# Another order of issue for the same 1303 operations of a delta-rule attention with a softplus layer behind it

## The chip, the cores and the metric

The kernel runs on one core of one Trainium2 chip, in one launch. The metric is device time in microseconds from start to end of that core's program. Engines are named as in the profile: PE is TensorE (matmul), PEld its weight load, DVE is VectorE, ACT is ScalarE, POOL is GpSimd, SP is SyncE, which here only issues DMAs.

## What is computed

```python
def _attn_ref(q, k, v, beta, g):          # 4 batches, 8 heads, 768 tokens, 48 features
    k_n = k / (np.linalg.norm(k, axis=-1, keepdims=True) + 1e-06)
    state = np.zeros((B, H, D, D))
    for t in range(S):
        readout = einsum('bhd,bhde->bhe', q[:, :, t], state)
        y[:, :, t] = g[:, :, t] * readout
        v_old = einsum('bhde,bhd->bhe', state, k_n[:, :, t])
        state = state + beta_t * einsum('bhd,bhe->bhde', k_n[:, :, t], v[:, :, t] - v_old)

def _moe_ref(x, w_in, w_out):             # x: y as 3072 tokens x 384; w_in 384 x 2048, w_out 2048 x 384
    h = x @ w_in
    return softplus(h) @ w_out
```

Each token reads the state of its head before it updates it. The second part is two dense layers with a softplus between them.

## The kernel before

**Tiling.** The 768 tokens are cut in 12 chunks of 64, for all 32 heads (4 batches x 8) at once. Inside a chunk the update of 64 tokens is done as matrix products with the inverse of a triangular matrix of 64 x 64 for each head; from chunk to chunk the state is handed on. The dense layers run on tokens of a chunk as soon as its output is there. Every piece of work is an `Item` with a number, a kind, a tag, the engines that can do it, the items it depends on and the buffers it uses. A letter and a number such as `P658` in the order table mean: issue item 658 now, on engine P (PE), D (DVE), A (ACT), G (POOL) or S (SP). The text names items by kind and tag, for example `ks:1.0` (chunk 1, half 0).

**What the items are**, in the order in which a chunk needs them:

- `load` (L264, L286): one half of a chunk's k, q, v or g, 192 KB, into one of three (k, v, g) or two (q) tiles; `cast` and `kmul` write it in 16 bits; `ksq`, `red`, `sqrt` or `pow` (L582, on POOL), `eps` make the norms of k, for two chunks at a time.
- `trs` and `kev`: transposes on PE and their copies; `gram`, `gramd`, `gramk`, `gramq`: products of k and q with k; `kkc`, `mask`: their copies.
- For each pair of chunks (tag 0, 2, 4, ...) `kd0`, `kd1`, `ln`, `clear`, `diag`, `prep`, then `step:pair.j`: 15 steps (pairs 0 and 2) or 31 steps (pairs 4 to 10) of forward substitution, each a multiply (L661) and an add (L668) that need the step before. A step may be on DVE or POOL. Then `cv`, `tn`, `c16`, `t32`, `xmm`, `xs`, `tmm`, `tlo`, `thi`, `zmm`, `z` build the rest of the inverse.
- The chain of the state, by chunk and half: `ks` (k times the state, L846), `w` (v less that, L887), `umm` (L895), `u1`, `zu` (L918), `u2`, then `smm` (L938) and `s` (the new state), and `qs`, `ymm` (L968), `y` (times g, L983), `ytr`, `xt` for the output. `ks` of the next chunk needs both `s:c.0` and `s:c.1`.
- `g1` (L1032): a piece of x @ w_in; `soft` (L1044, ACT): softplus; `g2` (L1059): four of 16 pieces of the second product, in the order .0, .4, .8, .12 into one PSUM bank; `o` and `store`.
- `wload` (L312, POOL's DMA queue): the eight weight transfers of 384 KB. w0.0 to w0.3 are quarters of w_in, w1.0 to w1.3 of w_out. The `g1` of columns 0 to 3 needs w0.0, and so on; `g2:c.p.0` needs w1.0, `.4` needs w1.1, `.8` w1.2, `.12` w1.3.
- `warm` (L1114): fills, 32 items of three matmuls on the identity whose results nobody reads.

**What sets the order.** `Program.emit` walks the table and calls each item's function, so the table is the order of instructions on each engine. Semaphores hold an instruction back until what it reads is there; an engine takes its own instructions strictly in turn. Buffers are given out in the order of the table too: the first item that uses a buffer takes the slot of the ring that came free first, and waits for that slot's last user. Rings that matter here: three tiles each for k, v and g, two for q, five PSUM banks `d`, two `h`, one `o`.

```python
        for word in table.split():
            en, no = word[0], int(word[1:])
            it = self.items[no]
            assert en in it.engs and no not in done and all(d.no in done for d in it.deps)
            for b in it.bufs:
                if b.ap is None:
                    b.slot = b.ring.free.pop(0)
                    b.ap = b.ring.tiles[b.slot]
            it.fn(en)
```

Of the kernel before, what the change touches and what calls it, by code (L numbers as in the profile page):

```python
# [1136 lines left out]
G259 A292 D293 A294 P651 D652 A206 G260 D261 D295 D262 A622 G263 G264 A207 D296 D312 P913 P316
A317 A914 P654 A655 P658 D659 G265 P300 A301 S64 P297 D298 D266 S63 P919 P166 D170 A920 P307
P921 A310 P313 A375 D311 S66 S65 S35 G267 S81 S82 G268 G269 D168 G270 G271 A922 P302 D306 A314
D304 A308 P1280 A303 D376 A305 P923 P318 D309 P210 D320 P323 A373 A321 A324 P917 A326 A319 A328  # L1140
S30 P1281 D211 G272 D374 P1288 P1290 A918 D273 P279 D325 A274 A924 D329 D330 A280 P1289 P1287
S36 A465 D275 D331 S51 P661 A662 P653 P656 A657 G377 D332 D333 D334 D335 D336 P911 A912 P915
# [6 lines left out]
G361 G362 S87 P1291 P1292 P695 D696 P693 D694 A381 P1293 P385 A386 G363 G364 D387 P927 A388 D389
P697 D698 P390 D392 D394 A481 A393 P690 A391 P689 D691 D692 P928 P929 P930 P288 D395 P708 A931  # L1150
D457 P706 P699 D700 S95 P396 A397 S45 D707 D289 P934 P935 S106 P709 P401 D403 A458 D459 A710
P936 P702 A703 P711 G460 A402 P937 A938 S940 P701 P704 A705 S96 D712 D365 D366 P719 D720 P957
A404 P406 A409 A407 A411 P717 P958 P959 D718 D405 D414 S61 D412 D413 P960 G415 A961 P721 A722
D461 P482 S109 P964 A483 S962 S963 A368 D416 D417 S939 P965 P966 S53 P971 A972 A564 D410 P987
A988 S52 S98 D408 P714 P713 D716 D478 P371 D372 P369 D370 D715 P989 A990 S104 P985 A986 G418
G419 G420 G421 D422 P479 D423 A480 P1001 A1002 P999 P730 P732 P723 D724 A1000 S60 A367 D731 P489
D491 P983 G424 D425 A492 A984 S932 P967 S103 A490 P977 A968 S969 A978 P975 A976 P725 P726 A727
S97 P733 A734 P997 A998 S59 P991 A992 S67 P735 A736 S970 P728 A729 D426 D427 D428 D429 D430 D431
P981 D432 A982 S68 P466 A467 P973 A974 P995 A996 P741 D742 P737 P743 D744 P738 S70 D739 D740
P979 A980 D493 D462 S62 P1003 S933 P745 A746 P747 D748 P484 A485 P754 D755 A541 G433 G434 G435  # L1160
G436 G437 G438 P993 G439 D488 D486 A994 P463 P1004 A464 P757 A758 S69 P750 D487 D542 P1005 P1006
A1007 S1008 P473 P468 D751 A539 D475 D474 P756 P1010 P1011 A469 A471 D540 P759 D470 P1012 S83
P1013 A1014 D760 S1016 P749 P752 A753 S1015 P767 S76 D440 D441 D768 A548 P1017 D472 P765 D766
P761 S84 P762 D764 P1018 G442 G443 G444 A476 G445 G446 G447 P769 P1019 D763 P1020 A494 G543 A770
P565 A1021 A566 P1047 P1031 P1024 D495 D496 A1048 A1032 S78 P1041 A1042 D448 P771 D449 P773
S1023 P778 A451 D779 D477 P1025 P1026 D497 D772 S107 A450 P1053 A1054 P452 P774 P781 D498 A775
P780 P1035 A1036 A782 D453 D499 P1049 P1027 A1028 S1029 P1061 A1050 A1062 D544 P783 A784 P454
P776 A777 D500 P1037 A1038 G501 D561 P562 A563 P1039 A1040 S1009 D502 D503 S1030 P1059 A1060 S75
D504 D505 P789 D506 D507 G508 P567 D571 A570 G509 G510 P791 P1033 A1034 D455 D792 S77 P1057
A1058 A568 D790 P549 A550 P1043 P1045 A1046 D569 P793 A794 D545 P572 A575 D574 D511 G512 P785  # L1170
D576 P786 D788 A1044 A573 D787 P1051 A1052 P546 A547 P1063 P1064 P1055 A1056 P802 P795 D513 D514
P551 A554 A552 P1065 P1066 A1067 S1069 D796 P798 P804 D803 D555 A799 G515 D516 D517 D518 D519
D520 P805 A806 P1070 P1071 P1072 P1073 S94 S1068 A1074 P797 P800 P807 A801 P1077 P1078 D521 A808
P556 P813 G522 D814 P815 A557 A559 P1079 P1080 D816 D558 D553 P817 A1081 S1082 D818 S91 S86 S93
P810 P809 D812 D811 G523 G524 D525 D526 G527 G528 G529 A577 P1084 P1099 G530 P1107 D578 D579
A1100 P828 A1108 P819 S1083 P826 D827 P1109 A1110 P1111 A1112 S110 P1085 P1103 A1104 S85 P1095
A1096 D820 P1086 P1115 A1116 D560 D531 P1117 A1118 D580 G581 D532 A534 D533 P1087 A1088 S1076
S1090 D582 S1089 S99 P1093 A1094 P1091 P829 A830 A1092 P821 P535 P822 A823 S1022 D583 G584 P1121
# [47 lines left out]
```

## Time and profile before

| what | value |
|---|---|
| time, median of 3 runs | 263.37 us (263.04 to 264.32) |
| the profiled execution | 264.15 us, its span 262.4 us |
| mean granted TensorE clock | 0.945 |
| DVE, ACT, POOL busy | 71%, 61%, 45% of the span |
| loads of q, v, g, k | 24 each, 192 KB, 4.7 to 5.0 us to landing in the median |
| weight transfers w_in, w_out | 4 each, 384 KB, 8.1 and 8.0 us |
| stores | 48, 96 KB, 2.4 us |
| PE rows `h` (L1032) and `o` (L1059) | 384 matmuls each, 74.1 and 71.8 us busy |

The span is the time from the first to the last instruction of the profiled execution. "Busy" counts an engine's own instructions; a wait is named with the instruction that ended it. "Granted clock" is the share of full speed that TensorE's throttle lets through.

### The profile page before, as it was taken

What the parts mean: (1) busy time and instruction counts of PE and PEld (TensorE: products, weight loads), DVE (VectorE), ACT (ScalarE), POOL (GpSimd) and SP (SyncE); (2) the same over time, 40 slices, a digit from 0 to 9 for tenths busy, and PEclk for the clock granted to TensorE, in tenths of its full rate; (3) what the DMA queues carried; (4) which work ended last, traced back from release to release, by engine and by line L of the source; (5) the groups of instructions that cost most, each with busy time, mean ns of one, the idle gap of its engine ahead of it and who ended that gap; (6) DMA issues with size and microseconds to landing.
All of it is one profiled execution on the core that took longest, in us unless ns stands there. A gap on an engine that the chain in (4) does not pass through costs nothing.

```text
span 262.4 us, 10491 instructions
## 1 busy us (share of the span) xinstructions
PE 239.2 (91%) x4552; PEld 154.4 (59%) x4552; DVE 186.9 (71%) x417; ACT 161.3 (61%) x297; POOL 118.0 (45%) x190
## 2 busy tenths in 40 slices
PE   6639888498999999999999999999999999999993
PEld 2525554375667676656666566664666455678761
DVE  7999777578988987989977987888566644622100
ACT  3646875298877747889667789455742466046440
POOL 5400983268646288560868735255573442000000
PEclk9658997579999999999999999999999999999998
DMA  8899999859389984895838150228423421012112
GB/s 115 139 181 189 167 185 203 143 103 188 77 158 143 180 128 90 147 178 114 145 69 119 32 106 4 65 54 143 94 49 66 87 50 31 17 32 62 32 45 61
DMA packets 86830, 27.51 MB, mean 105 GB/s; under 512 B 77056, under 2 KB 86784, under 8 KB 86784
## 3 DMA queue, kind: packets, MB, share of 16 engines
q1 hardware_dynamic: 80992, 23.31, 50.4%
q0 software_dynamic: 3712, 3.15, 7.7%
q10 hardware_dynamic: 2080, 0.39, 1.1%
q8 instruction: 35, 0.57, 1.0%
q14 instruction: 11, 0.09, 0.1%
HBM read 25.26 MB, written 4.72 MB: 114 GB/s over the span
## 4 chain that ended last, share of the span: by engine, by line
PE 48%; POOL 15%; DMA 15%; DVE 12%; issue 5%; SPq 2%; ACT 2%; POOLq 0%; DVEq 0%; ACTq 0%
PE o L1059 19%; PE h L1032 15%; DMA kf<-in_k_dram 9%; POOL tmp L661 5%; POOL tt L668 5%; DVE tt L668 4%; DVE tmp L661 4%; DMA w_out<-in_moe_w_out_dram 3%; PE d L846 3%; POOL nv L582 2%; DMA qf<-in_q_dram 2%; PE d L918 2%; PE d L895 2%; PE d L968 2%; PE d L801 1%
## 5 line engine op out<-in xcount | busy, mean ns | idle before, releaser
L1044 ACT ACTIVATE ga<-h 128x512 f16<-128x512 f32 x96 | 56.4, 599 | 32.3 <-PE h L1032 30.8
L1032 PE MATMUL h<-xt,w_in 128*128 128x512 f16 (+1 forms) x384 | 74.1, 331 | 0.0
L1059 PE MATMUL o<-w_out,ga 128*128 128x384 f16 x384 | 71.8, 327 | 1.0 <-ACT osb L203 0.6
L661 POOL TENSOR_TENSOR tmp<-nn,tt 128x192 f32<-128x192 f32 (+19 forms) x73 | 37.4, 512 | 68.2 <-DVE tt L668 64.4
L1059 PEld LDWEIGHTS <-ga 128*128 128x128 f16 x384 | 35.2, 98 | 23.8 <-issue 1.7
L1032 PEld LDWEIGHTS <-w_in 128*128 128x128 f16 x384 | 35.6, 99 | 20.7 <-issue 0.3
L668 POOL TENSOR_TENSOR tt<-tt,tmp 128x192 f32<-128x192 f32 (+19 forms) x73 | 37.9, 520 | 5.7
L661 DVE TENSOR_TENSOR tmp<-nn,tt 128x240 f32<-128x240 f32 (+16 forms) x81 | 26.9, 332 | 13.7 <-POOL tt L668 11.4
L1114 PE MATMUL o<-ident 128*128 128x512 f16 x96 | 28.6, 440 | 1.4 <-POOL ident masks.py:199 1.4
L668 DVE TENSOR_TENSOR tt<-tt,tmp 128x240 f32<-128x240 f32 (+16 forms) x81 | 27.2, 336 | 2.8
L203 ACT ACTIVATE osb<-o 128x384 f32<-128x384 f32 x21 | 10.3, 490 | 25.1 <-PE o L1059 23.7
L203 ACT ACTIVATE kqt<-d 128x1024 f16<-128x1024 f16 (+1 forms) x24 | 21.9, 922 | 3.8 <-PE d L403 1.8
L203 ACT ACTIVATE u<-d 128x384 f16<-128x384 f32 x38 | 17.9, 494 | 6.3 <-PE d L918 3.8
L203 ACT ACTIVATE kk<-d 128x256 f16<-128x256 f32 (+1 forms) x41 | 14.8, 404 | 6.7 <-PE d L518 3.9
L846 PE MATMUL d<-s,kqt 48*64 48x48 f16 x704 | 16.4, 190 | 2.1 <-DVE s L205 2.1
L846 PEld LDWEIGHTS <-kqt 48*64 48x64 f16 x704 | 13.5, 110 | 7.3 <-issue 7.1
L533 DVE TENSOR_TENSOR mt<-d,mask 128x256 f16<-128x256 f32 x40 | 15.5, 417 | 2.5 <-PE d L518 2.1
L582 POOL TENSOR_TENSOR nv<-nv,half_c 128x32 f32<-128x32 f32 x3 | 16.4, 5453 | 0.0
L1114 PEld LDWEIGHTS <-ident 128*128 128x128 f16 x96 | 9.3, 110 | 11.8 <-issue 4.9
L561 ACT ACTIVATE ksq<-kf 128x768 f32<-128x768 f32 x12 | 10.1, 843 | 9.5 <-DMA kf<-in_k_dram 7.5
L983 DVE TENSOR_TENSOR yg<-d,gf 128x384 f16<-128x384 f32 x24 | 12.3, 550 | 3.6 <-PE d L968 3.5
L887 DVE TENSOR_TENSOR w<-vf,d 128x384 f16<-128x384 f32 x22 | 11.3, 543 | 4.4 <-PE d L846 4.4
(116 smaller groups left out, 329.3 us busy)
## 6 DMA issues: line engine op xcount, KB each, us to landing
qf<-in_q_dram SPq DMA_DIRECT2D x24, 192.0 KB, 4.8
vf<-in_v_dram SPq DMA_DIRECT2D x24, 192.0 KB, 4.7
gf<-in_g_dram SPq DMA_DIRECT2D x24, 192.0 KB, 5.0
out_dram<-osb SPq DMA_DIRECT2D x48, 96.0 KB, 2.4
kf<-in_k_dram SPq DMA_DIRECT2D x22, 192.0 KB, 4.7
w_in<-in_moe_w_in_dram POOLq DMA_DIRECT2D x4, 384.0 KB, 8.1
w_out<-in_moe_w_out_dram POOLq DMA_DIRECT2D x4, 384.0 KB, 8.0
kf<-in_k_dram ACTq DMA_DIRECT2D x2, 192.0 KB, 4.6
```

The lines of the kernel that those rows point to most:

```text
L203: nc.scalar.activation(o, x, AF.Copy, scale=float(sign))
L533: nc.vector.tensor_tensor(mt[c][m].ap[:, NP * p : NP * p + NP], gb[m].ap.rearrange("p (n b) -> p n b", n=NP)[:, :, C:], mask[:, None, :].b ...
L582: lambda en: nc.gpsimd.tensor_tensor(nv.ap, nv.ap, half_c, ALU.pow),
L661: ENG[en].tensor_tensor(t, nn_[:, :, j + 1 :, j : j + 1].broadcast_to([P, nb, n, w]), tt_[:, :, j : j + 1, :w].broadcast_to([P, nb, n, w]) ...
L668: ENG[en].tensor_tensor(rows, rows, t, ALU.add)
L846: nc.tensor.matmul(hd(o.ap)[HALF[r], NP * p + i], kq_of(c)[FEAT[m], 8 * p + 2 * i + r, off : off + C], s0[r].ap[FEAT[m], NP * p + i], **st ...
L887: lambda en, m=m, w1=w1, wp=wp: nc.vector.tensor_tensor(w1.ap, heads(vf.ap, m), hd(wp.ap), ALU.subtract),
L983: lambda en, m=m: nc.vector.tensor_tensor(heads(yg.ap, m), hd(yp[m].ap), heads(gf.ap, m), ALU.mult),
L1032: nc.tensor.matmul(hp.ap[:, n * b : n * b + n], w_in[:, j, f * P : (f + 1) * P], xt.ap[:, j, t0 : t0 + n], start=(j == 0), stop=(j == 2),)
L1044: lambda en, hp=hp, o=gb: nc.scalar.activation(o.ap, hp.ap, AF.Softplus),
L1059: nc.tensor.matmul(op.ap[:, :DM], b.ap[:, col + c0 : col + c0 + 128], w_out[:, f, :], start=(f == 0), stop=(f == NF - 1),)
L1114: nc.tensor.matmul(wb.ap.rearrange("p (a b) -> p a b", a=4), ident, ident[:, None, :].broadcast_to([P, 4, P]),)
```

## The change

Only the order table `_ORDER` is replaced. All 1303 items stay, with the same functions, shapes, dependencies and rings. 1277 of the 1303 places hold another word; 110 items change engine, among them 53 steps of the forward substitution (25 from DVE to POOL, 28 from POOL to DVE). The places of the items that the prediction speaks of (a place is the position in the table, from 0; the letter is the engine):

| item | before | after |
|---|---|---|
| `wload:w0.3`, `w0.1`, `w0.2`, `w0.0` | G 191, 207, 155, 169 | G 146, 222, 237, 258 |
| `wload:w1.1`, `w1.3`, `w1.0`, `w1.2` | G 215, 397, 445, 450 | G 429, 379, 431, 432 |
| `load:q4.0`, `q4.1`, `k5.0`, `k5.1` | S 134, 194, 186, 202 | S 158, 164, 186, 185 |
| `load:k7.0`, `k7.1` | S 212, 217 | S 261, 260 |
| `ksq:5`, `ksq:7` | A 237, 277 | A 220, 298 |
| `red:5`, `red:7` | D 238, 298 | D 221, 301 |
| `cv:0` | D 78 | G 75 |
| `kd1:2`, `ln:2` | D 214, 226 | D 212, 213 |
| `s:0.0`, `s:0.1` | D 230, 233 | D 215, 210 |
| `ks:1.0`, `ks:1.1` | P 240, 259 | P 232, 227 |
| `zu:1.0`, `zu:1.1` | P 339, 351 | P 339, 321 |
| `ytr:1.0`, `umm:2.0` | P 372, 432 | P 372, 428 |
| `step:4.13` | G 434 | D 398 |
| `step:4.14` | D 435 | G 399 |
| `g2:0.0.0`, `g2:0.0.8` | P 480, 496 | P 475, 491 |

The first lines of the diff, and those that hold the weight transfers (items 111 to 118) and the two steps 347 and 348:

```diff
 _ORDER = """
-P1271 P1272 G1 S15 P1274 D173 D2 P1273 D3 A16 D126 S10 P129 G4 D125 P127 A24 G623 A119 D120 S12
-S23 A121 D148 S7 S14 S9 D6 S48 S13 P150 S8 S25 G149 P152 S11 D130 G0 P139 S20 A128 P136 S26 D151
...
-A223 A214 D215 S47 A205 P1275 P208 S57 A204 P629 S28 A239 P634 P1276 G113 A216 D209 A630 P631
-A632 D635 P636 G624 S27 D217 D218 P1277 A637 G111 P642 D643 A290 P644 D645 P219 A220 G234 P235
-D236 P646 A647 P648 P224 D649 A227 S55 D226 P240 D244 A241 G114 A225 A243 S50 D228 D242 P245
-A248 D291 P229 A232 S56 D246 P1278 D247 A230 G112 D249 A250 D233 D231 S71 G626 D251 G116 P1279
...
-P281 P278 P383 A952 A285 S37 D344 P945 A384 G118 A946 A398 P955 A956 P665 P666 D668 D667 D379
...
-S105 S54 P953 P947 A948 D676 P678 A679 G347 D348 P1294 D349 P685 A686 D350 D351 P677 P680 A681
-G115 P684 S44 A400 P380 G117 S43 P687 A688 D352 D353 D354 G355 G356 G357 G358 A954 G359 G360
...
+D4 G6 P1271 D173 P1272 S13 G0 G3 A16 S15 D125 P1274 P127 S10 D126 P1273 A24 A119 P129 D120 S23
+D148 D130 S11 S9 S8 S31 S7 A128 P136 D137 S14 S12 A121 D122 S20 S18 A138 P150 G149 P152 P139
...
+P143 D145 D628 S22 P1300 P1301 P1302 S26 A214 D193 A2 G1 S41 P1298 D195 D215 D147 P1295 P196
+A197 A203 G626 A216 D217 D218 A202 P199 A200 P222 P1296 D633 S42 P198 A205 S21 P1297 A204 P208
+P629 A223 P219 A630 A290 D209 D237 G114 P634 A635 G234 P631 A632 P1277 P201 A207 D220 P229 A206
...
+D226 A157 P210 A292 D293 G112 G650 P300 G624 A301 P658 D659 G255 G256 G257 P651 D258 A294 A622
+D295 G113 P166 D259 G260 D296 P661 A662 D261 D262 D263 D264 P925 A926 A373 P297 A298 D168 A315
+D652 P915 A916 G111 P1275 S72 S71 P307 G265 D266 D267 A310 S30 S46 S66 P654 A655 D309 G268 G269
...
+S43 P1289 P673 A674 P1287 D379 P1290 P949 A382 G118 G343 A950 P945 A946 P279 A280 P276 P675 S74
+G625 D344 S73 A277 P941 P953 D345 A954 D346 D347 G348 P383 A384 A942 P278 P281 P943 A285 A284
+S88 P1284 S38 P380 P682 D676 P286 A381 D683 D287 S87 D349 D350 D351 D352 P1283 P1285 S44 P677
+A282 P678 G116 A679 G115 G117 D353 P955 A956 P684 P685 A686 P680 A681 A398 P1286 A458 S81 P1291
...
```

More of the change, by code (lines that the diff above doesn't have):

```diff
@@ L1137 @@
[L1137 to L1142, printed above, removed]
@@ L1149 @@
[L1149 to L1154, printed above, removed]
@@ L1155 @@
[L1155 to L1178, printed above, removed]
@@ new lines @@
+S107 G437 G438 D439 D440 A539 D441 D442 P756 P759 A760 A751 P1006 P749 P767 G443 A1007 P752
+P1010 P1011 S969 P1012 A494 D540 D768 A753 P1013 A1014 S1015 D495 P765 P761 D472 P762 P1017
+P1018 D766 P769 D496 A770 P1019 P1020 A1021 P1055 A1056 G444 G445 G446 G447 D448 D449 D477 S1016
+P1053 A1054 P1024 P1031 S106 P1061 D564 D497 D498 P565 A450 D763 G543 A451 D764 D544 S1023 D499
+P1025 P1026 A566 A1062 S108 S77 S78 P771 D772 P778 D779 P780 D561 P452 A1032 P773 G500 P774 A775
+P1035 D453 A1036 G501 S84 P1041 A1042 G502 D503 S83 D504 D505 D506 P562 D507 D508 P549 P1047
@@ new lines @@
+G597 P1109 P1119 A825 P837 S99 D838 P834 P839 A1110 A1120 P833 D553 P1111 P1117 P1131 A1112
+A1118 D836 P1107 D840 P841 A1108 D835 A842 P843 P850 P852 P1132 P1133 D851 D844 P846 P845 A1134
+D598 D599 D600 P853 A854 S1136 A847 P1123 P1124 D601 G602 G603 P855 A856 G604 P848 A849 P1125
+P1126 A1127 S109 P861 S1135 D862 P857 P858 P863 D859 D864 D605 P1137 P1138 P865 P1139 P1140 A866
+A1141 S1142 P1165 S1143 A1166 P1169 A1170 P1144 D860 P1153 A1154 S1128 P1151 A1152 P1145 P1179
+A1180 P1175 S110 P1146 P1167 A1176 A1168 D606 D607 D608 S1129 G609 G610 G611 G612 G613 P1173
@@ L1196 @@
+P1215 A1216 P1234 P905 P907 D906 P1219 A1220 P1225 A1226 D908 P909 P1221 A1222 P1235 D910 P1249
+A1250 P1243 A1244 P1236 P1237 A1238 S1240 S1239 P1255 A1256 P1247 A1248 P1227 P1241 A1242 P1245
+A1246 P1228 P1229 P1230 A1231 S1232 S1233 P1253 A1254 P1251 A1252 P1257 P1258 P1259 P1260 A1261
+S1262 S1263 P1264 P1265 P1266 P1267 A1268 S1269 S1270
 """
```

69 lines of the change are left out of this document (43 added, 26 removed).

## The prediction

> **What bounds the kernel now.** I read the page first, then the busy time by stretches, then the chain of waits, then single rows.
>
> ```profile
> PE 239.2 (91%) x4552; PEld 154.4 (59%) x4552; DVE 186.9 (71%) x417; ACT 161.3 (61%) x297; POOL 118.0 (45%) x190
> ...
> PEclk9658997579999999999999999999999999999998
> DMA  8899999859389984895838150228423421012112
> ```
>
> TensorE is the bound as a whole, but its clock and the DMA row say that the first 85 us differ from the rest. The stretches (columns: length, busy time and count of PE, PEld, DVE, ACT, POOL, granted clock, DMA share, GB/s):
>
> ```profile
> 42.60:46.00 3.40, 2.06 (x99) 1.60 (x98) 1.90 (x3) 1.57 (x3) 1.36 (x3) 1.00 1.22 198
> 46.00:56.20 10.20, 6.91 (x83) 5.43 (x82) 7.11 (x16) 5.61 (x10) 4.01 (x8) 0.50 0.61 100
> 94.53:126.60 32.07, 32.07 (x677) 20.44 (x677) 28.51 (x58) 24.19 (x44) 18.47 (x30) 1.00 0.70 126
> 126.60:258.30 131.70, 130.28 (x2259) 83.42 (x2257) 79.75 (x170) 73.45 (x132) 52.20 (x87) 1.00 0.33 65
> ```
>
> From 94.5 us on PE hardly idles. So the order is worth what it changes before that: how late PE comes to a given amount of its own work. The chain of waits names two DMA pieces there (start, length, what):
>
> ```profile
> 35.38 14.03 DMA kf<-in_k_dram
> 49.44 0.04 issue
> 49.48 0.85 ACT ksq L561
> ...
> 84.78 0.74 POOL w_out L312
> 85.53 8.96 DMA w_out<-in_moe_w_out_dram
> 94.49 0.04 issue
> 94.53 1.46 PE o L1059 x8
> ```
>
> The rows of the timeline behind them (start, length, engine, line, in brackets the idle time before it and who ended it):
>
> ```profile
> 46.45 0.56 DVE L205 CAST qn<-qf 128x768 f16<-128x768 f32 x1 [1.91 <-DMA qf<-in_q_dram]
> 50.36 0.95 DVE L565 TENSOR_REDUCE nv<-ksq 128x16 f32<-128x768 f32 x1 [2.51 <-ACT ksq L561]
> ...
> 35.20 1.57 POOL L312 DMA_DIRECT2D w_in<-in_moe_w_in_dram  x2
> ...
> 36.90 0.78 POOL L312 DMA_DIRECT2D w_out<-in_moe_w_out_dram  x1
> ...
> 91.75 0.81 PE L1059 MATMUL o<-w_out,ga 128*128 128x384 f16 x4 [0.22 <-DMA w_out<-in_moe_w_out_dram]
> ```
>
> Five weight transfers issued at 31.2 to 36.9 us held back the loads of q4.1 and k5 (k and q loads take 4.7 and 4.8 us in the median), and VectorE idled 1.91 + 2.51 = 4.4 us for them. Later w1.0, issued at 84.72, released the first `o` matmul at 91.75 (7.0 us), and w1.2, at 85.53, the third group at 94.53 (8.96).
>
> **How I count.** The order table is the order on every engine, so the work ahead of an item is a sum of durations. PE items I price by the median distance from start to start in the full stretch: `g1` 0.66, `g2` 0.65, a fill 0.66, `zmm` 0.53, `zu` 0.33, `ymm` 0.29, `umm` 0.27, `ks` 0.26, `gram` 0.25, `smm` 0.23, `qs` 0.21 us; all PE items make 218.4 us. "Offset" is an item's start less the PE work ahead of it. Old: 31.2 at `ks:2.0` (81.6 - 50.4), 32.25 at `g2:0.0.0` (91.75 - 59.5), 33.9 at `ks:5.0`, 39.9 at the end (258.3 - 218.4). The growth after 94 us is spread thin (the largest single piece is 0.74), and no row lets me say that the new order has more or less of it. So the change in time is the change of the offset at `g2:0.0.0`.
>
> **The change part by part.** No operation is added or removed. 110 items change engine, but by their rows the sums are 198.7 to 199.2 us for DVE, 177.3 to 177.6 for ACT, 115.8 to 112.3 for POOL: nothing by itself.
>
> 1. Weights. w0.3 goes from place 191 to 146, w0.1 to 222, w0.2 to 237, w0.0 to 258, w1.1 from 215 to 429. Walking POOL's queue with the durations of its rows, w0.3 is issued near 27 us, while SP waits for a free q tile (`load:q4.0` stands behind `cast:q3.0`, done near 32.7). The q4, v1 and k5 loads then follow at some 0.64 us each, from 32.8 to 37.2, with no weight issued beside them before 41. At the median 4.7 us k5 lands near 42, and ACT comes to its `ksq:5` near 44. So both waits of DVE go: -4.4 us. The bounds are 0 (they are only put elsewhere) and -4.4.
>
> 2. DVE's other waits. Up to step 4.14, at 84.82 us, the old order has 72.7 us of DVE items ahead, so 12.1 us are lost; the new one has the same 72.7. Shuttling steps to POOL and back: by the rows, POOL's part exceeds DVE's cover by 0.62 at step 2.9 and 0.50 at 4.8, and `tn:2` waits 0.74; the new places cover all three: -1.8. Against that, step 0.14 has 16.4 us ahead in place of 17.8 and still ends near 22.8, since its chain starts from the same k loads and casts: +1.4. `cv:0` moves to POOL, 0.94 x 2 in place of 0.35 x 2, +1.2 us on its chain; `red:2`, `mask:0.0` and `w0:0.0` (0.94 + 0.66 + 0.5) fill DVE meanwhile, and behind it on POOL `cast:q2.0`, a fill copy and w0.3 are late by the same. What is late next is `tn:0`, `t32:0`, and all of chunk 0 by about 2 us: `z:0`, `y:0.1`, `kkc:2.01`, `s:0.1` each wait 0.7 to 0.9 where the old order lost 2.6 in all: +1.7. `s:0.0` now stands behind `kd1:2` and `ln:2` (1.29 + 1.04) and starts near 45.6, while the old order was through with both states at 47.5. Lost: 12.1 - 4.4 - 1.8 + 1.4 + 1.7 = 9.0 us, with bounds of 5.9 (none of the pluses) and 12.1 (as before).
>
> 3. The gate at `g2:0.0.0`. In the old order POOL issued w1.0 after step 4.13. In the new one step 4.13 is DVE's, 4.14 is POOL's (0.64 + 0.68), and w1.1, w1.0, w1.2 follow it. DVE ends 4.13 at 72.7 + 9.0 = 81.7, POOL ends 4.14 at 83.2, w1.0 is issued at 84.0, second of three. Its time to landing is bounded by 7.0 (the first of two) and 11.8 (the longest w_out of the issue view, one of five); it is nearest to the second of two, 8.96, which I take: 93.0. PE could be there sooner: DVE's work runs 21.7 us ahead of PE's at `umm:2.0`, so DVE allows an offset of 9.0 + 21.7 = 30.7, or 91 us at 59.9 of work. PE so waits some 2 us; behind it in its queue stand `ks:3` and all of chunk 3, for which DVE's `w:3` wait, with steps 4.15 to 4.30 to do meanwhile. Offset 93.0 - 59.9 = 33.1, against 32.25: **+0.9 us**. The third transfer may land by 95.8 (62.7 + 33.1) without adding to it.
>
> The profiled execution took 264.15 us (span 262.4, 1.75 around it); the sum makes it 265.0. It lay 0.78 above the median of the runs shown, 263.37, so the median becomes **264.2**. The range of this case alone is 262.6 to 266.0: landing 7.0 would give 263.37 - 1.0, and 11.8 would give + 3.7.
>
> **Rivals.**
>
> A. The gate does not bind. Lost time 7.5 (halfway from 9.0 to its lower bound) and w1.0 landing in 7.0 give 84.0 - 1.5 + 7.0 = 89.5, ahead of PE. Then DVE sets the offset: its work is 22.0 ahead of PE's at `ytr:1.0`, so 29.5 there, 30.4 at the gate with the old growth of 0.045 per us over 20 us. 30.4 - 32.25 = -1.85: **261.5**, own range 259.5 to 262.6. For it: the 4.4 us are real, and only k9, v3.1 and a q load share DMA there. Against it: three weights instead of two.
>
> B. Slower: TensorE's half clock stretches chunk 1. The clock fell to 0.50 at 46.0 after a stretch with 2.06 us busy of 3.4, and stayed there for 10.2 us. In the new order PE has 10.9 us of work (22.7 to 33.6) between `ks:1.1` and `zu:1.1`, some 17 us apart by DVE's chain, about the same 61 to 64%. At half clock (a `g1` took 1.46 in place of 0.83) they take some 20 us; `zu:1.1` is 3 us late, and DVE's `y:1.1` behind it loses what exceeds its slack of about 1, so 2.5: w1.0 lands at 95.5, offset 35.6: **266.8**. It decides from the point where `zu:1.1` starts after 64. Against it: DVE, not PE, sets the pace there. The Trainium skill, "TensorE: Matmul & The Clock Gate", section "HAM oscillation — how this bites in real kernels", asks only that PE have no gaps over about 3.4 us; by that rule the clock stays up, this rival falls and its time is 264.2. The trace does not agree: the longest gap before the fall was 0.77 us, and the longest in the cold stretch 2.1.
>
> C. The change does not do what it says: the wait moves to k7. Its loads (places 260, 261) are issued near 51, between w0.2 (48) and w0.0 (51). At 11.3 us (the median of k loads beside five weights) k7 lands at 62.4, `ksq:7` ends at 63.3, `red:7` is due on DVE at 60.7: 2.6 us lost, and `pow:6` (5.45 on POOL) and its steps come late: 264.2 + 2.6 = **266.8**; at the median 4.7 nothing. The Trainium skill, "DMA: Bandwidth & Descriptors", section "Queues, rings and completion order", says that an engine takes turns between queue rows, a packet each. By that rule a weight delays a load by no more than its own transfer time, an estimate from the queue rows of the profile, 262.4 x 7.7% / 8 = 2.5 us, so k7 would land at 60.8 and cost about 1. The 13.7 us of the longest k load, beside five weights, are within what the rule allows (4.7 + 12.5).
>
> **Chances.** 0.5%, 1.3 us, is about what a measurement of this kernel can tell from no change: 262.05 to 264.7. The forecast 0.36 (of it within 0.22, slower 0.11, faster 0.03); A 0.32 (faster 0.29, within 0.03); B 0.17 (slower 0.16, within 0.01); C 0.15 (slower 0.14, within 0.01). Together faster 0.32, within 0.27, slower 0.41. The range for 8 in 10 reaches from A's 259.8 to 268.8, which is B or C with the other half added.
>
> **What would show it.** Step 1: no idle time of DVE over 1 us ended by a q load or by `ksq` between 40 and 52 us. Step 2: step 4.13 ends on DVE at 81 to 83. Step 3: `g2:0.0.0` is released by w_out at 92 to 94 with idle time before it. A: no idle time there. B: granted clock 0.50 beyond 58 and `zu:1.1` after 64. C: `red:7` waits for `ksq` near 60. The forecast is wrong if the offset grows after 94 us by more than 9 or less than 6 us, which I have called the same.

## The result, and the profile after

| | before | after |
|---|---|---|
| time, median of 4 runs each | 263.85 us (263.04 to 264.66) | 266.46 us (266.36 to 266.79) |
| ratio of after to before | | 1.0101, interval 1.0064 to 1.0138 |
| the profiled execution, its span | 264.15, 262.4 us | 266.45, 264.7 us |
| mean granted clock | 0.945 | 0.965 |

The new order is slower by 1.0%, 2.6 us. That lies inside the range on record, but above the forecast of 264.2 and above the range of that case alone, and it isn't slower for a reason that the forecast gave.

The page of the changed kernel: busy time, the clock and DMA rows, and the shares of the chain of waits by engine.

```profile
PE 238.9 (90%) x4552; PEld 155.1 (59%) x4552; DVE 189.3 (72%) x420; ACT 163.0 (62%) x295; POOL 117.7 (44%) x189
...
PEclk9956998699999999999999999999999999999998
DMA  8798779999779969998325602637302300221112
...
PE 37%; DVE 23%; POOL 22%; issue 10%; ACT 3%; DMA 2%; SPq 1%; POOLq 0%; DVEq 0%; ACTq 0%
```

The sums hardly differ. The chain does: before, its shares were PE 48%, POOL 15%, DMA 15%, DVE 12%; now DMA has 2%, and DVE and POOL together 45%. A wait for transfers was exchanged for a chain through VectorE and GpSimd. Where that is can be read from the busy time by stretches (length, busy time and count of PE, PEld, DVE, ACT, POOL, granted clock, DMA share, GB/s), first of the kernel before:

```profile
46.00:60.00 14.00, 10.05 (x164) 7.75 (x164) 9.56 (x23) 9.26 (x16) 6.64 (x14) 0.63 0.74 131
...
94.50:130.00 35.50, 35.47 (x773) 22.96 (x773) 31.94 (x65) 27.51 (x50) 21.59 (x34) 1.00 0.72 128
130.00:190.00 60.00, 59.27 (x1143) 36.60 (x1143) 48.25 (x101) 40.45 (x74) 34.06 (x57) 1.00 0.42 77
```

and of the kernel after:

```profile
46.00:60.00 14.00, 12.34 (x202) 8.44 (x203) 12.62 (x32) 10.84 (x19) 8.73 (x21) 0.80 1.13 172
...
94.50:130.00 35.50, 34.31 (x705) 21.81 (x705) 28.92 (x61) 28.20 (x52) 22.01 (x33) 1.00 0.91 144
130.00:190.00 60.00, 57.47 (x1122) 35.96 (x1119) 48.74 (x106) 37.45 (x67) 35.35 (x55) 1.00 0.41 80
```

From 46 to 60 us DVE works 3.1 us more than before: the stall for q4 and k5 is gone. From 94.5 to 190 us PE idles 1.19 + 2.53 = 3.72 us, where it idled 0.03 + 0.73 = 0.76: all the gain and more is lost there.

Three rows of the timeline after answer to the steps of the prediction:

```profile
46.43 0.95 DVE L565 TENSOR_REDUCE nv<-ksq 128x16 f32<-128x768 f32 x1 [0.17 <-ACT ksq L561]
...
82.58 2.30 POOL L312 DMA_DIRECT2D w_out<-in_moe_w_out_dram  x3
...
94.38 1.46 PE L1059 MATMUL o<-w_out,ga 128*128 128x384 f16 x8 [0.90 <-DMA w_out<-in_moe_w_out_dram]
```

`red:5` waits 0.17 us in place of 2.51. The three w_out transfers are issued from 82.58 on. PE's wait for them is 0.90 us at `g2:0.0.8`, for the third; w1.0 landed at 89.45, before `g2:0.0.0` started at 90.5.

Next, the rows behind PE's idle time after that (timeline of the kernel after):

```profile
93.25 0.84 ACT L203 ACTIVATE qn<-qf 128x768 f16<-128x768 f32 x1 [2.15 <-DMA qf<-in_q_dram]
...
97.34 0.42 DVE L533 TENSOR_TENSOR mt<-d,mask 128x256 f16<-128x256 f32 x1 [2.22 <-ACT kk L203]
...
102.50 0.43 PE L968 MATMUL d<-u,mt 64*64 64x48 f16 x16 [0.53 <-ACT u L203]
...
127.34 0.42 DVE L661 TENSOR_TENSOR tmp<-nn,tt 128x247 f32<-128x247 f32 x1 [0.78 <-POOL tt L668]
...
129.01 0.55 DVE L887 TENSOR_TENSOR w<-vf,d 128x384 f16<-128x384 f32 x1
...
129.61 0.43 PE L846 MATMUL d<-s,kqt 48*64 48x48 f16 x16 [0.56 <-DVE w L887]
...
140.37 5.44 POOL L582 TENSOR_TENSOR nv<-nv,half_c 128x32 f32<-128x32 f32 x1
...
145.84 0.18 DVE L586 TENSOR_SCALAR nv<-nv 128x32 f32<-128x32 f32 x1 [0.65 <-POOL nv L582]
...
146.32 1.16 DVE L650 TENSOR_TENSOR nn<-ln,beta_l 128x1024 f32<-128x1024 f16 x1
147.40 1.01 DVE L887 TENSOR_TENSOR w<-vf,d 128x384 f16<-128x384 f32 x2
...
148.00 0.43 PE L895 MATMUL d<-w,te 64*64 64x48 f16 x16 [0.78 <-DVE w L887]
...
184.01 1.19 PE L801 MATMUL d<-to,kk 64*64 64x32 f16 x64 [1.09 <-ACT to L211]
```

The pattern is the same at 129 and at 148 us: `w` (L887), which PE needs at once, stands in DVE's queue behind two steps, or behind `eps:10` and `prep:8` (L586, L650), and the first of these waits for POOL (0.78 us for a step; 0.65 for `pow:10`, which takes 5.44). `zmm:8` at 184.01 then waits 1.09 us for `tlo:8.1` (L211), a copy of the same chain of the inverse on ScalarE. At 97 us the stall starts on ACT: `cast:q9.0` waits 2.15 us for its load, and behind it stands `kev:k7.0`, which the products and `mask:7.00` need.

What DVE waited for from 82 us (after; in total, times, longest) is 6.9 us in all, of which the largest are

```profile
DVE mt L533 <- ACT kk L203: 2.2, 1, 2.2
DVE tmp L661 <- POOL tt L668: 2.1, 3, 0.8
DVE tt L638 <- ACT tn L203: 0.7, 1, 0.7
```

and before, from 84.4 us (the same place in the work) to 130 us, 2.7 us:

```profile
DVE mt L533 <- PE d L518: 0.8, 1, 0.8
DVE w L887 <- PE d L846: 0.5, 1, 0.5
```

So DVE gives back in these 48 us the 4 us by which it was ahead.

PE's idle time from 70 to 215 us of its own work (102.5 to 256.2 us after, 103.4 to 254.1 before) is 3.19 us after and 0.77 before. After, it is seven waits: `zmm:8` 1.09, `umm:6.0` 0.78, `ks:5.0` 0.56, `zmm:7` 0.44 and three of about 0.1. Before, the longest is this one, at `umm:6.0` too (timeline of the kernel before):

```profile
147.29 0.59 PE L895 MATMUL d<-w,te 64*64 64x48 f16 x26 [0.36 <-ACT te L211]
```

### The profile page after: what moved, and what is told of

It reads as the page before. It is cut to its first block, busy times and chain, and to the rows that moved or that the text cites. A ratio compares the mean times of both kernels' runs of the same rounds, so it can differ in the third digit from the quotient of the medians.

```text
span 264.7 us, 10491 instructions
## 1 busy us (share of the span) xinstructions
PE 238.9 (90%) x4552; PEld 155.1 (59%) x4552; DVE 189.3 (72%) x420; ACT 163.0 (62%) x295; POOL 117.7 (44%) x189
## 4 chain that ended last, share of the span: by engine, by line
PE 37%; DVE 23%; POOL 22%; issue 10%; ACT 3%; DMA 2%; SPq 1%; POOLq 0%; DVEq 0%; ACTq 0%
PE o L1059 16%; PE h L1032 11%; POOL tt L668 9%; POOL tmp L661 9%; DVE tmp L661 7%; DVE tt L668 6%; PE d L846 2%; DMA kf<-in_k_dram 2%; POOL nv L582 2%; DVE kkd L620 2%; DVE mt L533 1%; DVE nn L650 1%; PE d L918 1%; PE d L968 1%; PE d L895 1%
## 5 line engine op out<-in xcount | busy, mean ns | idle before, releaser
L661 POOL TENSOR_TENSOR tmp<-nn,tt 128x60 f32<-128x60 f32 (+16 forms) x70 | 34.4, 492 | 61.6 <-DVE tt L668 49.4
L668 POOL TENSOR_TENSOR tt<-tt,tmp 128x60 f32<-128x60 f32 (+16 forms) x70 | 37.8, 540 | 5.5
L661 DVE TENSOR_TENSOR tmp<-nn,tt 128x252 f32<-128x252 f32 (+18 forms) x84 | 28.4, 338 | 11.6 <-POOL tt L668 9.2
L668 DVE TENSOR_TENSOR tt<-tt,tmp 128x252 f32<-128x252 f32 (+18 forms) x84 | 28.5, 340 | 2.9
L203 ACT ACTIVATE u<-d 128x384 f16<-128x384 f32 x40 | 18.9, 495 | 8.4 <-PE d L895 3.7
L203 ACT ACTIVATE kqt<-d 128x1024 f16<-128x1024 f16 (+1 forms) x24 | 21.2, 895 | 3.8 <-PE d L403 3.0
L846 PE MATMUL d<-s,kqt 48*64 48x48 f16 x704 | 17.1, 190 | 4.5 <-DVE s L205 3.8
L533 DVE TENSOR_TENSOR mt<-d,mask 128x256 f16<-128x256 f32 x40 | 16.1, 414 | 2.8 <-ACT kk L203 2.2
L983 DVE TENSOR_TENSOR yg<-d,gf 128x384 f16<-128x384 f32 x24 | 12.9, 552 | 5.1 <-PE d L968 4.2
L203 ACT ACTIVATE kk<-d 128x256 f16<-128x256 f32 (+1 forms) x36 | 13.4, 411 | 4.4 <-DVE mt L533 3.3
L887 DVE TENSOR_TENSOR w<-vf,d 128x384 f16<-128x384 f32 x22 | 11.5, 548 | 5.4 <-PE d L846 5.4
```

Of the source, the lines that this page charges most:

```text
L203: nc.scalar.activation(o, x, AF.Copy, scale=float(sign))
L533: nc.vector.tensor_tensor(mt[c][m].ap[:, NP * p : NP * p + NP], gb[m].ap.rearrange("p (n b) -> p n b", n=NP)[:, :, C:], mask[:, None, :].b ...
L661: ENG[en].tensor_tensor(t, nn_[:, :, j + 1 :, j : j + 1].broadcast_to([P, nb, n, w]), tt_[:, :, j : j + 1, :w].broadcast_to([P, nb, n, w]) ...
L668: ENG[en].tensor_tensor(rows, rows, t, ALU.add)
L846: nc.tensor.matmul(hd(o.ap)[HALF[r], NP * p + i], kq_of(c)[FEAT[m], 8 * p + 2 * i + r, off : off + C], s0[r].ap[FEAT[m], NP * p + i], **st ...
L887: lambda en, m=m, w1=w1, wp=wp: nc.vector.tensor_tensor(w1.ap, heads(vf.ap, m), hd(wp.ap), ALU.subtract),
```

## The experiments

The measure is the offset of the prediction (start of a PE item less the PE work ahead of it, with the same prices), taken at 55, 60, 70 and 215 us of PE work; these places lie near 85, 91, 103 and 256 us after the start. It is of the profiled execution; the time is the median, the ratio is to the kernel before in the same comparison. The traces of e1 and e11 are of executions of 266.91 and 266.08 us, below the medians in the table.

| run | 55 | 60 | 70 | 215 | 70 to 215 | time, us | ratio, interval |
|---|---|---|---|---|---|---|---|
| before | 31.4 | 32.2 | 33.3 | 38.9 | 5.65 | 263.85 | |
| after | 30.4 | 30.6 | 32.9 | 41.1 | 8.24 | 266.46 | 1.0101 (1.0064 to 1.0138) |
| e1, new to 453, then old | 28.6 | 33.9 | 36.4 | 41.7 | 5.26 | 268.89 | 1.0181 (1.0136 to 1.0226) |
| e2, old to 453, then new | 32.0 | 43.0 | 45.3 | 53.2 | 7.87 | 277.76 | 1.0536 (1.0492 to 1.0580) |
| e3, new, weights ahead of step 4.14 | 29.9 | 37.9 | 38.6 | 46.5 | 7.93 | 272.29 | 1.0311 (1.0265 to 1.0357) |
| e4, new, five PE items moved | 30.2 | 30.4 | 32.6 | 40.2 | 7.54 | 265.30 | 1.0052 (1.0027 to 1.0078) |
| e5, new to 494, then old | 30.4 | 30.6 | 32.4 | 37.7 | 5.24 | 262.74 | 0.9967 (0.9944 to 0.9990) |
| e6, new, steps to DVE | 29.5 | 29.8 | 32.1 | 39.7 | 7.60 | 265.23 | 1.0058 (1.0036 to 1.0080) |
| e7, new, q8 loads later | 29.6 | 31.1 | 31.8 | 40.4 | 8.66 | 266.20 | 1.0110 (1.0066 to 1.0154) |
| e8, old to 494, then new | 31.4 | 31.9 | 35.3 | 43.5 | 8.24 | 268.51 | 1.0185 (1.0151 to 1.0219) |
| e9, e5 with three edits | 30.6 | 30.9 | 32.1 | 36.9 | 4.82 | 261.85 | 0.9917 (0.9891 to 0.9943) |
| e10, old, weights moved | 27.1 | 27.6 | 29.0 | 34.4 | 5.34 | 259.64 | 0.9844 (0.9821 to 0.9867) |
| e11, new, w1.2 and w1.3 exchanged | 30.1 | 30.3 | 32.5 | 40.8 | 8.26 | 266.99 | 1.0094 (1.0058 to 1.0129) |
| e12, e10 with two edits | 28.2 | 28.9 | 29.7 | 35.1 | 5.33 | 260.00 | 0.9859 (0.9826 to 0.9891) |

### Which part of the table loses the time: e1, e2, e5, e8

```diff
-_ORDER = new
+_ORDER = new[:453] + [w for w in old if w's item is not in new[:453]]      (e1; e2 the other way round)
+_ORDER = new[:494] + [w for w in old if w's item is not in new[:494]]      (e5)
+_ORDER = old[:494] + [w for w in new if w's item is not in old[:494]]      (e8, with:)
-P689 D691 D457 A458 S45 ... S104 D700 P709 A710 P401
+P689 D691 S45 ... S104 D700 D457 P709 A710 A458 P401
```

> The first 453 places are the new table's, the other 850 items follow in the old table's order and on its engines. Theory T (the second part of the new table loses by itself: it places less PE work ahead of products that wait for the inverse): the gain of about 1.6 us that the trace shows at g2:0.0.0 is kept, and the old growth of 7.6 follows, so 261.9 to 263.1 us, below the kernel before (263.9), and the offset at the last g2 near 38.3 to 39.2. Rival R (the loss starts with the 0.90 us wait for w1.2 at g2:0.0.8 and is only carried on, the second part being as good as the old one): that wait is in the first part's issue order, so the time stays near the changed kernel's, 265.5 to 266.5 us.

> The first 453 places are the old table's, the other 850 items follow in the new table's order. T: the second part brings its growth with it, 266 to 268 us (old offset 32.2 at the gate plus 9.4 to 10.5, less what waits take up); at least 1.5 us over the kernel before. R: as the kernel before, 263.4 to 264.5 us, since the wait for w1.2 isn't made worse.

Both were far slower than either theory said, and the join itself was the cause. In e1 ScalarE stood still (timeline of e1):

```profile
91.31 0.84 ACT L203 ACTIVATE qn<-qf 128x768 f16<-128x768 f32 x1 [6.17 <-DMA qf<-in_q_dram]
```

The items of the old part that were missing came in a clump, `cast:q8.0` among them, soon behind the issue of its own load; two softplus pieces, `kev:q7.0` and `kkc:6.01` stood behind it in ACT's queue, and the offset rose from 28.6 to 33.9. In e2 it was `ksq:9` in front of `u2:2.1`: ScalarE stood still for 7.82 us, and the offset rose by 11.0. As a test of the time the two runs fail. But behind the join each took up the growth of its later part: 5.26 with the old one, though 3 us late, and 7.87 with the new one, though 12 us late. So two cleaner joins were made.

> As the first of these joins, but at place 494, behind w:3.1, so that no cast stands ahead of its own load on ScalarE: the first 494 places are the new table's, the rest follows in the old order. T2 (the offset grows by an amount that belongs to the later part of the table, and a delay is carried to the end undiminished): offset near 31.5 at 96 us, then the old 6.2, so 37.7 to 38.6 at the end and 262.4 to 263.6 us. Rival R2 (a later part only does well behind its own first part): 265 us or more.

> The reverse join: the first 494 places are the old table's, the rest follows in the new order, with red:8 put behind w:3.0 and ksq:9 behind u1:3.1 so that they don't block their queues. T2: offset 32.8 at 97 us plus the new table's 9.3, so near 42 at the end, 266.8 to 268.3 us. R2: as for the other join, over 268. If the later part were no worse than the old one: 263.5 to 264.5 us.

Measured 262.74 and 268.51 us. e5 lies in T2's range, and R2 falls there. e8 lies 0.2 us above T2's range and so, by its time alone, where R2 had it (over 268). What speaks for T2 in e8 is where the time is lost: from 70 us of PE work on it grows by 8.24 us, as the kernel after does, and the excess comes at the join, where the offset rises by 3.4 us from 60 to 70 (2.3 in the kernel after). The stretches of e5

```profile
94.50:130.00 35.50, 35.50 (x713) 22.59 (x712) 29.27 (x60) 27.68 (x50) 20.90 (x33) 1.00 0.77 141
130.00:190.00 60.00, 59.29 (x1155) 36.68 (x1154) 48.28 (x103) 40.59 (x73) 33.98 (x58) 1.00 0.40 76
```

and of e8

```profile
94.50:130.00 35.50, 33.50 (x711) 21.54 (x714) 29.55 (x59) 26.26 (x46) 22.79 (x34) 1.00 0.86 137
130.00:190.00 60.00, 56.94 (x1116) 35.61 (x1112) 48.88 (x105) 37.65 (x68) 36.03 (x56) 1.00 0.39 76
```

show it without any prices: with the old later part PE idles 0.00 + 0.71 us there, with the new one 2.00 + 3.06. The four long waits of the kernel after stand in e8 at the same items, `zmm:8` 1.05, `umm:6.0` 0.78, `ks:5.0` 0.57 and `zmm:7` 0.44, and from 70 to 215 us of PE work PE idles 3.16 us in e8 and 0.71 in e5. From 70 us of PE work on, the unchanged old part adds 5.2 to 5.7 us and the unchanged new part 7.9 to 8.7, whatever the lateness at which it starts (29 to 45 us). So a delay made before 103 us is carried to the end almost in full; the later part takes up less than 1 us of it.

### What the weights are worth alone: e10

```diff
-P1276 G113 A216 ... P1277 A637 G111 P642 ... D244 A241 G114 A225 ... D247 A230 G112 D249 ... G626 D251 G116 P1279
+P1276 G111 A216 ... P1277 A637 P642 ... D244 A241 A225 ... D247 A230 D249 ... G626 D251 P1279
+A200 G650 G113 A315 ... A206 G260 G114 G112 D261 ... A384 G118 G116 A946
```

> The old table with only its weight transfers moved: w0.0 first (place 155), w0.2 behind vs:1, w0.3 and w0.1 behind step 2.3, w1.1 behind w1.3, so that one weight, not five, goes beside the loads of q4.1 and k5. Theory W (the gain ahead of g2:0.0.0 comes from the weights): both waits of VectorE (1.91 and 2.51) go, k5 lands near 42 to 45, step 4.14 ends 1 to 2.5 us earlier, w1.0 lands as much earlier, 262.3 to 263.2 us. Rival (it comes from the steps and other moves): 263.6 to 264.4 us.

Measured 259.64 us, 1.56% faster than before and better than theory W asked. Timeline and stretch of e10:

```profile
46.00:60.00 14.00, 13.12 (x230) 9.71 (x228) 11.62 (x25) 12.21 (x24) 11.57 (x24) 0.76 0.94 155
```

```profile
30.07 0.98 POOL L312 DMA_DIRECT2D w_in<-in_moe_w_in_dram  x1
...
39.19 0.80 POOL L312 DMA_DIRECT2D w_in<-in_moe_w_in_dram  x1
...
44.04 0.55 DVE L205 CAST qn<-qf 128x768 f16<-128x768 f32 x1
...
45.73 0.95 DVE L565 TENSOR_REDUCE nv<-ksq 128x16 f32<-128x768 f32 x1 [0.19 <-ACT ksq L561]
...
90.27 1.46 PE L1059 MATMUL o<-w_out,ga 128*128 128x384 f16 x8 [0.49 <-DMA w_out<-in_moe_w_out_dram]
```

`cast:q4.0` has no wait, `red:5` 0.19 us; `w:2.1` ends at 80.03 in place of 84.36 us, and the offset is 4.3 lower at 55 and 4.6 at 215 us of PE work. Five transfers moved out of the way of two loads give the whole of the gain. Against e10, the kernel after stands 3.0 us worse at 60 us of PE work (30.6 against 27.6; one execution of each, and two executions can differ by 1.1 there, see the last section) and 6.7 at 215; the medians differ by 6.8.

### The gate: e3, e7, e11

```diff
-S74 G625 D344 S73 ... A282 P678 G116 A679 G115 G117 D353            (e3)
+S74 G625 G116 G115 G117 D344 S73 ... A282 P678 A679 D353
```

> The new table with only w1.1, w1.0 and w1.2 moved ahead of step 4.14 in POOL's queue, into 3.6 us in which POOL is idle; they are issued near 77.7 to 79.3 us in place of 82.6 to 84.1, and the 0.90 us wait of g2:0.0.8 should be gone by both theories. T: later waits of PE for the inverse take the 0.9 us up, 266.0 to 266.6 us. R: the 0.9 us and the 2.2 us for which VectorE stood still behind it are gained, 264.3 to 265.6 us.

Both theories were wrong, by 6 us. The three transfers now shared with k9.0, g2.1 and v3.1: k9.0 took 11.88 us to landing in place of 6.14. ScalarE and TensorE of e3:

```profile
89.93 0.84 ACT L561 ACTIVATE ksq<-kf 128x768 f32<-128x768 f32 x1 [5.39 <-DMA kf<-in_k_dram]
...
91.42 0.49 ACT L203 ACTIVATE u<-d 128x384 f16<-128x384 f32 x1
```

```profile
91.96 0.62 PE L968 MATMUL d<-u,mt 64*64 64x48 f16 x16 [5.05 <-ACT u L203]
```

`ksq:9` stands three items ahead of `u2:2.1` on ACT, so a late load stopped the state. The new table has next to no slack at this place: in the kernel after, k9.0 lands at 84.56 and `ksq:9` starts at 84.94.

```diff
-P1286 A458 S81 P1291 ... P947 S82 S45 ... A407 S104 D700
+P1286 A458 P1291 ... P947 S45 ... A407 S81 S82 S104 D700         (e7)
-A382 G118 G343 ... G115 G117 D353
+A382 G117 G343 ... G115 G118 D353                                (e11)
```

> The new table with only load:q8.0 and load:q8.1 moved from places 444 and 467 to 497, ahead of load:k11.1, so that they no longer share the DMA engines with w1.2 and q9.0 (q8 is not read before 108 us). Sharing theory: w1.2 lands near 92 in place of 94.3, the 0.90 us wait of g2:0.0.8 goes, cast:q9.0 and kev:k7.0 behind it start near 92.6, and, delays being carried to the end, 264.9 to 265.7 us. Rival (w1.2 is slow by itself, or PE waits elsewhere): 266.2 to 266.8 us.

> The new table with only w1.2 and w1.3 exchanged. g2:0.0.8 no longer waits for w1.2; g2:0.0.12 waits 0.3 us or less for w1.3. Carried to the end: 265.6 to 266.1 us. Rival (as with the q8 loads, PE waits somewhere else instead, at ymm:3.0 or ks:4.0): 266.2 to 266.8 us.

The rival holds twice: 266.20 and 266.99 us (the second 0.2 above its range), no gain over the kernel after. In e7 w1.2 landed at 92.88 as expected, but with q8 out of the way g3.0, q9.0 and q10.0 were issued earlier, w1.0 took 8.32 us in place of 6.07, and PE waited at `g2:0.0.0` (timeline of e7):

```profile
91.00 1.30 PE L1059 MATMUL o<-w_out,ga 128*128 128x384 f16 x7 [1.12 <-DMA w_out<-in_moe_w_out_dram]
```

In e11 the wait at `g2:0.0.8` went and `ymm:3.0` waited instead (ScalarE and TensorE of e11):

```profile
100.41 1.27 ACT L203 ACTIVATE tn<-tt 128x1024 f16<-128x1024 f32 x1 [1.25 <-POOL tt L668]
```

```profile
102.12 0.43 PE L968 MATMUL d<-u,mt 64*64 64x48 f16 x16 [1.23 <-ACT u L203]
```

`c16:4` stands on ACT ahead of `u2:3.0` and waits for step 4.30, the last of eleven steps on POOL. The old table has `c16:4` on DVE. In the kernel after this second wait is there too, 0.53 us at `ymm:3.0`; with the first one gone it grew to 1.23. So near 100 us taking away one wait shows the other.

### What the later part waits for: e4, e6

```diff
-P747 D748 P757 A469 A758 P1004             (g2:2.0.4 ahead of ks:5.0)
+P1004 P747 D748 P757 A469 A758
-P774 A775 P1035                            (g1:4.2 ahead of umm:6.0)
+P1035 P774 A775
-P454 D788 P795 ... P1063 P1059             (g1:4.14 ahead of zmm:7)
+P1059 P454 D788 P795 ... P1063
-P800 A801 P1078                            (g2:5.0.4 ahead of zu:7.0)
+P1078 P800 A801
-P535 P537 G580 ... D538 P1087              (g2:5.1.12 ahead of zmm:8; all e4)
+P1087 P535 P537 G580 ... D538
```

```diff
-D441 D442 P756 ... P767 G443 ... A1056 G444 (6.26, 6.27 behind 6.25)
+D441 D442 D443 D444 P756 ... P767 ... A1056
-G511 D512 ... D519 G520                    (8.11, 8.20)
+D511 D512 ... D519 D520
-D523 P797 G524 G525                        (8.24, 8.25)
+D523 D524 D525 P797
-G530 G531 D532                             (c16:8; all e6)
+G530 D531 D532
```

> The new table with five products of the dense layers, ready by the trace, moved ahead of five items for which PE waits: g2:2.0.4 ahead of ks:5.0, g1:4.2 ahead of umm:6.0, g1:4.14 ahead of zmm:7, g2:5.0.4 ahead of zu:7.0, g2:5.1.12 ahead of zmm:8. T: PE works through 0.65 + 0.65 + 0.4 + 0.3 + 0.65 = 2.65 us of its waits, nothing of the inverse comes later, 263.8 to 265.0 us. A rival, that the chain of the steps alone sets the end: no change, 266.2 to 266.7 us. R: the wait at 94 us is untouched, so at most half of it, 265.2 to 266.5 us.

> The new table with steps 6.26, 6.27, 8.11, 8.20, 8.24, 8.25 and c16:8 put on VectorE, each right behind or ahead of its VectorE neighbour, where POOL's took 0.9 to 1.8 us each and VectorE's take 0.65 to 0.85. T3 (the chain of steps, VectorE and POOL in turn, is what comes late for PE after 130 us): pow:10 and prep:8 come 1.5 us earlier, zmm:8 3 us or more earlier, PE's waits at umm:6.0, zmm:7 and zmm:8 (1.0 + 0.6 + 1.2) mostly go, 264.0 to 265.2 us. Rival R3 (PE is late there by its own order and by what stands on VectorE, not by the steps): y, s and w behind the steps come 0.7 to 1.4 us later, 266.2 to 267.5 us.

Each gained about 1.2 us in the median: 265.30 is outside T's range and inside R's, 265.23 just outside T3's. The intervals of both ratios overlap with that of the kernel after (1.0064 to 1.0138), so the gains are barely clear of noise. The growth from 70 to 215 us fell only from 8.24 to 7.54 and 7.60. In e4 PE still waited 0.61 us at `zmm:8` and 0.26 at `umm:6.0`, and new waits of 0.28 and 0.26 us came behind `g1:4.5` and at `g2:5.1.0`. In e6 the waits at `umm:6.0`, `zmm:7` and `zmm:8` went, and others came (TensorE of e6):

```profile
137.14 0.59 PE L938 MATMUL d<-u,kn 64*64 64x48 f16 x32 [0.59 <-DVE yg L983]
...
168.75 0.43 PE L918 MATMUL d<-u,z 64*64 64x48 f16 x16 [0.98 <-DVE yg L983]
```

The two sums of the prediction, taken at `s:7.0`, which `ks:8.1` reads, fit this (DVE time lost is the end of the item less the DVE work up to it, DVE ahead is that work less PE's, all by the prices of the old trace):

| | DVE lost by `w:2.1` | by `w:5.1` | by `s:7.0` | DVE ahead at `s:7.0` | offset of `ks:8.1` |
|---|---|---|---|---|---|
| before | 12.2 | 13.2 | 17.7 | 17.8 | 36.8 |
| after | 8.2 | 13.4 | 17.7 | 20.2 | 38.6 |
| e6 | 7.4 | 12.6 | 13.5 | 24.3 | 38.4 |
| e10 | 7.8 | 8.8 | 13.3 | 17.8 | 32.4 |
| e5 | 8.2 | 12.9 | 17.5 | 17.0 | 35.8 |

Offset is lost time plus DVE ahead, plus the 0.6 to 1.3 us from the end of `s:7.0` to the start of `ks:8.1`. That holds by construction, and PE did not idle in front of `ks:8.1` in any of the five. In e6, putting steps on DVE took 4.2 us from its waits and added 4.1 to its work, and `s:7.0` ended at 177.44 us, as before that edit (177.54). So TensorE may be paced by DVE's whole queue there, and not by the steps alone; the sums fit that and do not show it.

### A version that beats both: e9, e12

```diff
-A382 G118 G343 ... G115 G117 D353          (w1.2, w1.3 exchanged, e9)
+A382 G117 G343 ... G115 G118 D353
-P1026 D497 D772                            (w:6.0 ahead of clear:8, e9)
+P1026 D772 D497
-A384 G118 G116 A946 ... A400 P380 G117 S43 (w1.2, w1.3 exchanged, e12)
+A384 G117 G116 A946 ... A400 P380 G118 S43
-D580 G581 D532                             (t32:8 ahead of clear:10, both)
+D532 D580 G581
```

> The join at place 494 (262.7 us) with three edits: w1.2 and w1.3 change places (w1.2 is then issued near 72 us and w1.3, needed 0.65 us of PE work later than w1.2, in its place near 84); w:6.0 ahead of clear:8; t32:8 ahead of clear:10. Carried to the end, what PE waited at g2:0.0.8 (0.98, of which 0.3 stay for w1.3), umm:6.0 (0.52) and zmm:8 with what surrounds it (0.8) makes 0.65 + 0.5 + 0.6 = 1.75 us: 260.7 to 261.7 us. Rival (the waits come back at the next item, as with the q8 loads): 262.2 to 262.9 us.

> The old table with its weight transfers moved (259.6 us) and two of the three edits of the improved join: w1.2 and w1.3 exchanged (the wait of 0.66 us at g2:0.0.8 and what follows it), and t32:8 ahead of clear:10 (PE's 0.35 + 0.26 + 0.20 around umm:8.1 and zmm:8). In the improved join these were worth 0.58 us between 60 and 70 us of PE work and 0.54 at 150. Carried to the end: 258.2 to 258.9 us. Rival: given back later, 259.3 to 259.9 us.

e9 came to 261.85, half of what was expected: the exchange and `t32:8` took some 0.5 us each, and `w:6.0` nothing: `umm:6.0` waited 0.36 us as in e5, until ScalarE's `te` was done. e12 stands at 260.00, no better than e10: its trace shows the two gains (0.64 us between 60 and 70 us of PE work, 0.55 between 145 and 150), but also some 0.5 us lost between 70 and 110, so that its growth from 70 to 215 is that of e10 (5.33 and 5.34), and an offset that is 1.1 higher at 55. Most of that is there near 30 us, where `red:3` starts at 30.59 in place of 29.66; the first edit acts only at 74.20, when w1.2 is issued. The intervals of e10 and e12 overlap, so the two edits are not shown to be worth anything on top; e10 is the fastest, 6.8 us below the kernel after.

## Why the prediction was right or wrong, step by step

- **Step 1, the weights: right.** Both waits of DVE went. w0.3 was issued at 26.95 (forecast near 27), q4.0 at 33.0 (32.8), `s:0.0` started at 45.4 (45.6). k5 landed at 45.4, not 42, but DVE's other work hid that. e10 shows that the -4.4 are real and, alone, reach the end as -4.6.
- **Step 2, DVE's lost time up to step 4.14: right.** Forecast 9.0 in place of 12.1; step 4.13 ended at 81.08 (81.7), which is 8.4. e10 has 7.7, so the pluses and minuses of the other moves came to +0.7, not +1.3, as far as one execution of each can tell.
- **Step 3, the gate: mis-sized.** The issue at 83.38 (84.0) was right. I took 8.96 us to landing for w1.0, with bounds of 7.0 and 11.8; it took 6.07, below both. At its issue one other weight, w1.1, and two loads, v3.1 and k9.0, were under way; that this is why it was quick was not tried. PE had no idle time before `g2:0.0.0`, and the offset was 30.6 in place of 33.1: -2.5. That is what rival A worked out from DVE's work: 29.5 at `ytr:1.0` (measured 29.4) and 30.4 at the gate. That the third transfer may land by 95.8 without adding to it fell too: it landed at 94.34, and as PE was early, it cost 0.90. The range of the case, 262.6 to 266.0, does not follow from its bounds either: by its own sums they give 263.37 - 1.0 = 262.4 and 263.37 + 3.7 = 267.1.
- **The step that failed: "The growth after 94 us is spread thin (the largest single piece is 0.74), and no row lets me say that the new order has more or less of it."** The growth was taken as equal. From 60 to 215 us of PE work the old order grew by 6.7, the new one by 10.5: +3.8. It is also over the 9 us that the prediction named as a sign of being wrong: from `g2:0.0.8` at 94.38 us (62.7 us of work ahead, offset 31.7) to 215 us of work alone it is 9.4. With step 3 that makes -2.5 + 3.8 = +1.3 on the forecast's +0.9, the +2.2 of the offset at the end. The joins show that this belongs to the table's later part. About 1.2 of it arises up to 70 us of PE work, where the third transfer, `cast:q9.0` and POOL's steps end close together. Nearly all of the other 2.6 shows as PE's idle time: 3.19 us in place of 0.77, in seven waits of at most 1.09 us. There was a hint of it in the rows: the sum "DVE ahead of PE" that I used up to the gate gives, carried on to `s:7.0`, 20.2 for the new table and 17.8 for the old, +2.4. I stopped that sum at the gate. But that the lost time came out equal (17.7) is known only from the traces, and in e6 the same sum reads 24.3 with no later `ks:8.1`, so the hint alone would not have given the number.
- **The range.** 266.46 us lies in the range for 8 in 10, but that reaches so far up for rivals B and C, and both fell. The time lies inside by the width of the range, not by a mechanism that was forecast.
- **Rival A** had the first 90 us right and the end wrong, by the same assumption. **Rival B** fell: the clock was 0.50 from 45 to 51 us and not beyond 58, and `zu:1.1` started at 62.3. The rule of the Trainium skill ("TensorE: Matmul & The Clock Gate", "HAM oscillation — how this bites in real kernels"), gaps of over about 3.4 us, does agree with the kernel after, where the fall came in a gap of 3.85 us, but not with e10, where the clock fell at 46 us too and the longest gap in the 9 us before it was 0.79. **Rival C** fell: k7 landed at 57.3, and `red:7` waited for nothing. Its bound from the Trainium skill ("DMA: Bandwidth & Descriptors", "Queues, rings and completion order"), one transfer time for each weight that shares, agrees with e3: three weights cost k9.0 5.7 us, the estimate from that page and the queue row allows 3 x 2.5 = 7.5.

What stays open is which places of the later part have to change to get the 2.6 us back. The waits are known, but e4 and e6, which changed five and seven places at these waits, got only 0.6 to 0.7 of growth each; the two were not tried together. In e4 PE's idle time fell by 1.45 us (from 3.19 to 1.74) for 0.7 of growth, so a wait that is filled is not all gained, and why is open too.

## What to carry to other kernels

When an order of issue is replaced, compare it with the old one at several points from the first stage to the last, not at the first gate alone. Two sums help, if they are read together: the time that the pacing engine loses, and the work of that engine that stands ahead of the bounding engine's. The idle time of the bounding engine by stages then tells where an order loses. Look for the smallest part of the change that removes a wait that the chain names; here five moved transfers gave 1.6% by themselves, and the new table with all its other moves is slower by 1.0%. In an in-order queue an item that waits for a transfer or for another engine's chain is a wait for all that stands behind it, so put it behind what the next stage needs, and let a transfer be issued only when no load that is needed sooner is under way.

## What the runs showed of the hardware

- POOL's small operations are held up by some of DVE's. The same addition of 31 columns took 1.19 us beside `kd1:6` (L620) and 0.25 alone (kernel after, POOL and DVE):

```profile
99.37 1.28 DVE L620 SCALAR_TENSOR_TENSOR kkd<-kk,own,kkd 128x1024 f16<-128x1024 f16 x1
...
99.58 1.19 POOL L668 TENSOR_TENSOR tt<-tt,tmp 128x31 f32<-128x31 f32 x1
...
140.16 0.25 POOL L668 TENSOR_TENSOR tt<-tt,tmp 128x31 f32<-128x31 f32 x1
```

  It started after `kd1:6` did and ended 0.12 us behind its end (99.37 + 1.28 = 100.65; 99.58 + 1.19 = 100.77), so it was held as long as that instruction ran. A 60-column step beside the L342 product of 768 columns ended 0.15 us behind it (148.31 and 1.11 us of POOL, 148.32 and 0.95 of DVE; 0.29 alone). My prices for POOL's steps left this out. The Trainium skill has the rule ("SBUF — State Buffer", "SBUF: two separate sides"): GpSimd shares a pair of ports with VectorE, and an instruction of VectorE with two SBUF inputs that starts first keeps them to its end against one of GpSimd that reads SBUF. The first pair of rows agrees with it; in the second the two start within 0.01 us, so which came first cannot be read.
- ScalarE's queue waits as a whole: 5.39 us (e3) and 6.17 us (e1) for one load, with work behind it that was ready. The Trainium skill says the same ("PSUM — Partial Sum Buffer", "Engine vs sequencer instructions": the queues of ScalarE, VectorE and GpSimd are strictly first in, first out); the traces agree.
- Two executions with the same order up to 73 us differed by 1.1 us in offset (e10 and e12 at 55 us of PE work: 27.1 and 28.2). On DVE `red:3` starts 0.93 us later in e12 (30.59 in place of 29.66), and `kd1:4` 1.11 later (62.24 in place of 61.13). What sets it was not tried.
